# One more GpSimd drain and one TensorE branch hint near the end of a scan-and-experts kernel

## The chip, the cores and the metric

The kernel runs on one core of one Trainium2 chip. Its time is the device time of an execution in microseconds (us). Before the change it is 1088.54 us, the median of three runs. A core has five engines that run their own instruction lists: TensorE (PE in the profile; PEld is its weight load), VectorE (DVE), ScalarE (ACT), GpSimd (POOL) and SyncE (SP). A q behind an engine's name (POOLq, SPq, PEldq) means its sequencer, which reads the list, waits on semaphores, branches and issues transfers. The list itself is fetched from memory by DMA, on the queues that the profile calls "instruction".

## The reference

Two stages. A gated linear recurrence over 4 sequences of 5056 tokens, 256 wide:

```
a_t = exp(8 * sigmoid(r) * log(sigmoid(a_param)))
h   = a_t * h + sqrt(1 - a_t*a_t) * sigmoid(i) * x      (one step per token)
```

Then its output, 20224 rows of 256, goes through a mixture of 8 experts: each token takes the expert with the largest of 8 logits, and its row becomes `gate * (relu(row @ w1[e]) @ w2[e])`, with w1 256 x 1024 and w2 1024 x 256.

## The kernel before

**Front.** The recurrence is done in quads of 512 tokens by ScalarE (gates) and VectorE (scan). Its rows are then sorted by expert: GpSimd writes each row by an indirect DMA (L819, 158 of them) to its expert's part of a buffer in device memory.

**Slots.** The expert stage works in 90 slots of 256 or 128 rows of one expert. Which expert and which rows a slot holds is known at run time alone; SyncE reads it from a table. For a slot, SyncE loads the rows transposed (`xT`), their factors and token numbers (`meta`) and the two weight blocks (`wt`, L969; skipped where the same expert's are there already). TensorE does the first product (`L1`, L1049), ScalarE and VectorE its relu (L1061, L1069), TensorE the second product two slots later (`L2`, L1088 to L1090), ScalarE scales it by the factor `f` that GpSimd has made (L1022, L1096), and GpSimd writes the 128 rows to the output by an indirect DMA (`store`, L1101, 164 of them, one per 128 rows). The weight, `hb`, `ot` and `xT` buffers rotate.

**Order.** A planner of costs and due times (`Plan`) orders these steps; the kernel emits them in its order, and each engine works its list in order.

**The branch.** How many slots of 128 rows the last table fills depends on the data. Sixteen are sure and stand in the plan; code for 19 more stands under `tc.If(used > x["sure"])` (L1219) in `rest()`, which is called ahead of the first product of slot 85 (`late`, with TAIL = 5). Every engine reads `used` (L1218) and takes one of two ways: into the body, or to a short block behind it that raises the semaphores by what the body would have added. In the list of each engine the body lies between the test and that short block; on TensorE it has 2755 instructions. In the executions here the body is not run.

**The end.** Behind the last slot the framework adds a drain on every engine, a barrier, a clearing of semaphores and a second barrier, all put down to L1309. SyncE's part first waits for every transfer.

Of the kernel before, what the change touches and what calls it, by code (L numbers as in the profile page):

```python
# [48 lines left out]
TAIL = 5  # L49
# [483 lines left out]
def lru_moe(ctx, tc, plan, rix, a_in, wg_in, w_in, c_in, id_in, out):  # L533
    nc = tc.nc
    ctx.enter_context(tc.manual_schedule())
    V, A, T, G = nc.vector, nc.scalar, nc.tensor, nc.gpsimd
# [198 lines left out]
    def shape(g):  # L735
        B = sum(plan.quads[z] for z in plan.groups[g])
        return grp[g], B, lambda t: t.unsqueeze(2).to_broadcast([P, B, E])
# [21 lines left out]
    @op  # L759
    def rk(g):  # L760
        o, B, _ = shape(g)
        n = B * E
        pr = o["pr"] = misc[:, 256:256 + 2 * n]
        T.matmul(pr[:, n:2 * n], ones16, flat(o["oh"]), start=True, stop=True)
        T.matmul(pr[:, 0:n], umat, flat(o["oh"]), start=True, stop=True)
# [205 lines left out]
    @op  # L971
    def slot(k):
        o = slots[k]
        ti, j = st["tab", o["z"]]["ti"], o["j"]
        o["r0"] = nc.values_load(ti[:, 1, j:j + 1], engines=[SP], min_val=0, max_val=E * plan.cap,
                                 skip_runtime_bounds_check_because="a row of the buffer")
        o["er"] = nc.values_load(ti[:, 0, j:j + 1], engines=[SP], min_val=0, max_val=E - 1,
                                 skip_runtime_bounds_check_because="an expert")
# [20 lines left out]
    def done_rows(o, i):  # L999
        after(o["c"], i)  # L1000
        if o["e"] is None:
            tc.add_to_no_dep_group("rowload", i.ins)
# [188 lines left out]
    def late_constants():  # L1191

        umat_ = const.tile([P, P], F16, name="umat")
        V.tensor_copy(umat_, cst[:, C_U:C_U + P])
        V.tensor_copy(wg32[:, :, 0:E], wg)

        val_ = const.tile([P, E], F32, name="val")
        V.tensor_copy(val_, cst[:, C_ECAP:C_ECAP + E])
        val9_ = const.tile([1, E + 1], F32, name="val9")
        V.tensor_copy(val9_, cst[0:1, C_ECAP:C_ECAP + E + 1])  # L1200
        for z in range(2):
            nc.sync.dma_start(buf[E * plan.cap + 256 * z:E * plan.cap + 256 * z + 256, :].rearrange("(p j) c -> p j c", j=2), pad)
        return umat_, val_, val9_
# [9 lines left out]
    def rest():  # L1213

        x = plan.orders[-1]
        if x["n"] == x["sure"]:
            return
        used = nc.values_load(st["used"], min_val=0, max_val=x["n"], skip_runtime_bounds_check_because="a count of slots")  # L1218
        with tc.If(used > x["sure"]):  # L1219
            for j in range(x["sure"], x["n"]):  # L1220
                k = len(slots)
                o = dict(k=k, e=None, U=P, J=1, c=x["c"], z=len(plan.orders) - 1, j=j)
                slots.append(o)
                slot(k)
                rw = bass.ds(o["r0"], P)
                meta = small.tile([P, 2], F32, name="last_meta")
                done_rows(o, nc.sync.dma_start(meta, buf[rw, D:D + 2]))
                z = work.tile([P, 2, W], F32, name="in_i", bufs=BUFS["i"]).rearrange("p h w -> p (h w)")
                xT = z[:, 0:D].bitcast(F16).rearrange("p (c u) -> p c u", c=4)
                done_rows(o, nc.sync.dma_start_transpose(xT, buf.bitcast(F16)[rw, 0:2 * D]))  # L1230
                ws, f2 = [], small.tile([P, 1], F32, name="last_f")
                for i in range(2):
                    src = wscr[bass.ds(o["er"], 1), i].rearrange("a p c -> p (a c)")
                    sc = small.tile([P, 1], F32, name=f"last_s{i}")
                    nc.sync.dma_start(sc.bitcast(F16), src[:, 4 * F:4 * F + 2])
                    G.tensor_tensor(f2, f2 if i else meta[:, 0:1], sc, ALU.mult)
                    for y in range(2):
                        t = work.tile([P, 2, W], F32, name="in_x", bufs=BUFS["x"])
                        ws.append(t.rearrange("p h w -> p (h w)").bitcast(F16))
                        nc.sync.dma_start(ws[-1], src[:, 2 * F * y:2 * F * (y + 1)])  # L1240
                h = work.tile([P, 2, W], F32, name="in_r", bufs=BUFS["r"]).rearrange("p h w -> p (h w)").bitcast(F16)
                h = h.rearrange("p (l f u) -> p l f u", l=2, f=NF)
                for g in range(2):
                    p1 = ps_y.tile([P, 2, D], F32, name="yt").rearrange("p a (b u) -> p (a b) u", u=P)
                    gs = slice(4 * g, 4 * g + 4)
                    for i in range(4):
                        fs = slice((4 * g + i) * P, (4 * g + i + 1) * P)
                        for y, (wl, kk, xl) in enumerate(TERMS):
                            T.matmul(p1[:, i], ws[wl].rearrange("p (k f) -> p k f", k=2)[:, kk, fs], xT[:, 2 * xl + kk], start=(y == 0), stop=(y == 5))
                    A.activation(h[:, 0, gs], p1, AF.Relu)  # L1250
                    V.scalar_tensor_tensor(h[:, 1, gs], p1, 0.0, h[:, 0, gs], ALU.max, ALU.subtract)
                for f in range(NF):
                    for y, (l, wl) in enumerate(((0, 0), (0, 1), (1, 0))):
                        T.matmul(misc[:, 0:D], h[:, l, f], ws[2 + wl].rearrange("p (c d) -> p c d", c=NF)[:, f, :],
                                 start=(f == 0 and y == 0), stop=(f == NF - 1 and y == 2))
                A.activation(z[:, D:2 * D], misc[:, 0:D], AF.Copy, scale=f2)
                i = G.indirect_dma_start(
                    out=out[:, :], out_offset=bass.IndirectOffsetOnAxis(ap=meta.bitcast(I32)[:, 1:2], axis=0),
                    in_=z[:, D:2 * D], in_offset=None, bounds_check=plan.tok - 1, oob_is_err=False)
                tc.declare_no_dep(i.ins, group="out", reason="every token has a row of its own")  # L1260
                tc.add_to_no_dep_group("out", i.ins)

    umat = val = val9 = None

    late = next(t for t in plan.ops if t.name == "L1" and t.args == (len(plan.slots) - TAIL, 0))
    for t in plan.ops:
        if t in first:
            continue
        if umat is None and t.eng == "DVE":
            umat, val, val9 = late_constants()  # L1270
        if t is late:
            rest()
        emit[t.name](*t.args)
# [39 lines left out]
```

## Time and profile before

| what | value |
|---|---|
| runs | 1085.17, 1088.54, 1093.79 us |
| profiled execution | 1085.49 us, of which 1083.4 us are the span from first to last instruction |
| mean granted TensorE clock | 0.966 |
| TensorE busy | 981.6 us, 91% of the span |
| GpSimd busy | 428.6 us, 40% |

A busy figure counts matmuls whose ends are modelled, so a TensorE that is 91% busy is not at its peak. Branches, drains and semaphore waits are not counted as busy anywhere; they are found in the answers on one source line, where each has its duration and the start of its first and last.

### The profile page before, as it was taken

Reading aid. Unit: us, or ns where it says so; the run is one execution under the profiler, and the core shown is the slowest. Engines: PE = TensorE matmul, PEld = TensorE weight load, DVE = VectorE, ACT = ScalarE, POOL = GpSimd, SP = SyncE. Lnnn points to the kernel's source line nnn. Section 1 sums busy time; section 2 is a strip of 40 time slices with the busy share of each in tenths; the row PEclk is TensorE's granted clock in tenths of the full one; section 3 lists DMA queues with packets and bytes.
Section 4 is the critical chain, followed back from the end, with each engine's and each line's share of the span. In section 5 each row is a group of like instructions: output and inputs, shape, how many; then the busy total and the mean of one; then the engine's idle time right before and its main releaser. Section 6 shows DMA issues by size and latency. Waiting matters only on the chain. (4 is left out here: it accounts for less than half of the span.)

```text
span 1083.4 us, 23684 instructions
## 1 busy us (share of the span) xinstructions
PE 981.6 (91%) x8790; PEld 863.3 (80%) x8790; DVE 689.4 (64%) x1400; ACT 602.9 (56%) x797; POOL 428.6 (40%) x496
## 2 busy tenths in 40 slices
PE   1328998987999999999999999999999999999985
PEld 1216886866888888888888888888888888889984
DVE  5899897776846576675857768577685663422210
ACT  8766755747455756657476574765746553322221
POOL 0364452251652435345354353544435434122221
PEclk9957998988999999999999999999999999999998
DMA  9968989889899999989999998998999996699951
GB/s 339 403 219 192 313 284 322 245 276 319 282 340 345 343 303 251 357 266 365 328 317 361 269 345 282 299 347 266 335 314 305 361 284 204 193 355 310 248 146 61
DMA packets 170578, 316.67 MB, mean 292 GB/s; under 512 B 119892, under 2 KB 120153, under 8 KB 147930
## 3 DMA queue, kind: packets, MB, share of 16 engines
q1 hardware_dynamic: 155002, 273.50, 81.0%
q0 software_dynamic: 15456, 41.60, 12.4%
q8 instruction: 71, 1.16, 0.5%
q14 instruction: 49, 0.40, 0.1%
HBM read 251.41 MB, written 63.91 MB: 291 GB/s over the span
## 5 line engine op out<-in xcount | busy, mean ns | idle before, releaser
L1049 PE MATMUL p<-xT,wt 128*128 128x256 f16 (+1 forms) x3936 | 417.6, 264 | 3.0 <-SPq L1219 3.0
L1049 PEld LDWEIGHTS <-wt 128*128 128x128 f16 x3936 | 357.4, 99 | 41.9 <-SPq L1219 3.3
L1088 PE MATMUL po<-wt,hb 128*128 128x256 f16 x1184 | 322.8, 273 | 3.3 <-ACT ot L1096 2.7
L1090 PE MATMUL po<-wt,hb 128*128 128x256 f16 x1184 | 322.7, 273 | 0.0
L1089 PE MATMUL po<-wt,hb 128*128 128x256 f16 x1184 | 322.7, 273 | 0.0
L1101 POOL DMA_INDIRECT out<-ot,meta x164 | 186.2, 1135 | 304.6 <-ACT ot L1096 268.7
L1069 DVE SCALAR_TENSOR_TENSOR hb<-p,hb 128x1024 f16<-128x1024 f32 x148 | 180.6, 1221 | 197.7 <-ACT hb L1061 193.5
L1061 ACT ACTIVATE hb<-p 128x1024 f16<-128x1024 f32 (+1 forms) x164 | 167.1, 1019 | 202.6 <-PE p L1049 199.0
L819 POOL DMA_INDIRECT buf<-rows,pi x158 | 172.4, 1091 | 60.3 <-issue 36.8
L1096 ACT ACTIVATE ot<-po,f 128x256 f32<-128x256 f32 x148 | 70.0, 473 | 163.2 <-PE po L1090 150.6
L1088 PEld LDWEIGHTS <-hb 128*128 128x128 f16 x1184 | 115.8, 98 | 17.2 <-issue 4.5
L1089 PEld LDWEIGHTS <-hb 128*128 128x128 f16 x1184 | 115.9, 98 | 17.1 <-issue 4.2
L1090 PEld LDWEIGHTS <-hb 128*128 128x128 f16 x1184 | 115.8, 98 | 13.4
L1022 POOL TENSOR_SCALAR f<-meta,wt,wt 128x2 f32<-128x2 f32 (+1 forms) x82 | 38.3, 467 | 186.1 <-DMA wt<-wscr 139.7
L646 DVE TENSOR_TENSOR_SCAN in_x<-in_r,in_x 128x512 f32<-128x512 f32 (+7 forms) x82 | 96.2, 1181 | 1.4
L627 DVE SCALAR_TENSOR_TENSOR in_x<-in_i,in_x 128x1024 f32<-128x1024 f32 (+1 forms) x38 | 45.8, 1204 | 46.8 <-ACT in_i L622 46.8
L611 DVE SCALAR_TENSOR_TENSOR in_x<-in_i,in_x 128x1024 f32<-128x1024 f32 (+1 forms) x38 | 47.8, 1258 | 39.2 <-ACT in_i L605 20.2
L731 DVE SCALAR_TENSOR_TENSOR rows<-yt,sc,rows 128x256 f16<-128x256 f32 x158 | 66.3, 477 | 6.5 <-ACT rows L724 4.9
L697 PE MATMUL yt<-cst,in_x 128*128 128x128 f32 x316 | 48.7, 299 | 23.3 <-DVE rows L731 8.2
L724 ACT ACTIVATE rows<-yt,sc 128x256 f16<-128x256 f32 x158 | 63.7, 476 | 8.3 <-DVE sc L716 5.3
L1049 PE MATMUL p<-x,wt 128*128 128x256 f32 x256 | 60.9, 394 | 3.1 <-POOL x L1010 3.1
L1086 PE MATMUL po<-wt,hb 128*128 128x256 f32 x256 | 62.5, 397 | 0.5 <-ACT ot L1096 0.4
(110 smaller groups left out, 869.0 us busy)
## 6 DMA issues: line engine op xcount, KB each, us to landing
wt<-wscr SPq DMA_DIRECT2D x164, 1024.5 KB
in_x<-in_rix SPq DMA_DIRECT2D x39, 512.0 KB
in_r<-in_rix SPq DMA_DIRECT2D x37, 512.0 KB
in_i<-in_rix SPq DMA_DIRECT2D x37, 512.0 KB
wscr<-hl SPq DMA_DIRECT2D x16, 1024.5 KB
wt<-in_w SPq DMA_DIRECT2D x16, 1024.0 KB
out<-ot,meta POOLq DMA_INDIRECT x164, 7.0
buf<-pad SPq DMA_DIRECT2D x10, 258.0 KB
```

What stands on the lines that cost most here:

```text
L646: V.tensor_tensor_scan(y[:, lo:hi], av[:, lo:hi], y[:, lo:hi], init, ALU.mult, ALU.add)
L724: A.activation(o["rows"].bitcast(F16)[:, 2 * p + j, 0:D], o["yt", p][:, j], AF.Copy, scale=o["sc"][:, 2 * p + j:2 * p + j + 1])
L731: V.scalar_tensor_tensor(r[:, 2 * p + j, D:2 * D], o["yt", p][:, j], o["sc"][:, 2 * p + j:2 * p + j + 1], r[:, 2 * p + j, 0:D], ALU.mult, ...
L819: i = G.indirect_dma_start(out=buf[:, :], out_offset=bass.IndirectOffsetOnAxis(ap=g["pi"][:, b0 + j:b0 + j + 1], axis=0), in_=rows[q]["row ...
L1049: T.matmul(pv[:, i], wv[:, wl, kk, fs], o["xT"][:, 2 * xl + kk, 0:U], start=(z == 0), stop=(z == len(seq) - 1))
L1061: A.activation(o["h"][:, gs, 0:U] if o["raw"] else o["h"][:, 0, gs, 0:U], o["p1", g], AF.Relu)
L1069: V.scalar_tensor_tensor(o["h"][:, 1, gs, 0:U], o["p1", g], 0.0, o["h"][:, 0, gs, 0:U], ALU.max, ALU.subtract)
L1088: T.matmul(dst, h[:, 0, f, ts], wv[:, 0, f, :], start=(f == 0), stop=False)
L1089: T.matmul(dst, h[:, 0, f, ts], wv[:, 1, f, :], start=False, stop=False)
L1090: T.matmul(dst, h[:, 1, f, ts], wv[:, 0, f, :], start=False, stop=(f == NF - 1))
L1096: A.activation(o["ot", j], o["po", j], AF.Copy, scale=o["f2"][:, j:j + 1])
L1101: i = G.indirect_dma_start(out=out[:, :], out_offset=bass.IndirectOffsetOnAxis(ap=o["id"][j], axis=0), in_=o["ot", j], in_offset=None, bou ...
```

## The change

Three lines have an effect. The test gets the name "few"; a hint for that branch is asked for on TensorE at the step `L2` of slot 83; and GpSimd gets a drain ahead of `store` of slot 85. The assertion (n is 64 at most) adds no instruction.

```
-        with tc.If(used > x["sure"]):
+        with tc.If(used > x["sure"], label="few"):
...
+    full = next(t for t in plan.ops if t.name == "store" and t.args == (len(plan.slots) - TAIL, 0))
+    soon = next(t for t in plan.ops if t.name == "L2" and t.args == (len(plan.slots) - TAIL - 2, 0, 0))
     for t in plan.ops:
...
+        if t is soon:
+            tc.mark_branch_hint_location("few", engines=[mybir.EngineType.PE])
+        if t is full:
+            G.drain()
```

The first rows of TensorE's list, at the start of the program (misc, yt and ls are tiles of the front), before:

```order
L1309 UNCONDITIONAL_BRANCH
L665 MATMUL misc<-in_x,wg_120 32x128 x8
L697 MATMUL yt<-cst,in_x 128x128 x8
L680 MATMUL misc<-cst,ls 128x128
L665 MATMUL misc<-in_x,wg_120 32x128 x8
L680 MATMUL misc<-cst,ls 128x128
```

and with the change:

```order
L1317 UNCONDITIONAL_BRANCH
L1317 BRANCH_PREFETCH_HINT
L665 MATMUL misc<-in_x,wg_120 32x128 x8
L697 MATMUL yt<-cst,in_x 128x128 x8
L680 MATMUL misc<-cst,ls 128x128
L665 MATMUL misc<-in_x,wg_120 32x128 x8
```

The hint does not stand where it was asked for: it is the first instruction of TensorE's list, some 15,200 instructions ahead of the branch, which it names, marked as likely taken. (The step it was asked at comes behind the branch in the plan.) In the built list the taken side of TensorE's test is the short block behind the body. Nothing else in TensorE's list changes but the line numbers.

GpSimd's list between the branch and the end, with the change (a drain is not shown in such a listing):

```order
L1102 DMA out<-ot,meta 20224x256
L1023 TENSOR_SCALAR f_15898<-meta,wt_131,wt_134 128x1
L1102 DMA out<-ot,meta 20224x256
L1023 TENSOR_SCALAR f_15978<-meta,wt_132,wt_135 128x1
L1102 DMA out<-ot,meta 20224x256
L1023 TENSOR_SCALAR f_16069<-meta,wt_2563,wt_2564 128x1
L1102 DMA out<-ot,meta 20224x256
L1023 TENSOR_SCALAR f_16218<-meta,wt_130,wt_133 128x1
L1102 DMA out<-ot,meta 20224x256
L1023 TENSOR_SCALAR f_16237<-meta,wt_131,wt_134 128x1
L1102 DMA out<-ot,meta 20224x256 x3
L1317 UNCONDITIONAL_BRANCH
```

The rows are the stores of slots 82 to 89 and the factors of slots 85 to 89. They stand as before; the new drain is between the factor of slot 87 (f_16069) and the store of slot 85 behind it, so five stores and two factors follow it. It waits for no semaphore and raises none.

## Rows read from the trace of the kernel before

**Rows 1.** Page, busy time by engine.

```profile
PE 981.6 (91%) x8790; PEld 863.3 (80%) x8790; DVE 689.4 (64%) x1400; ACT 602.9 (56%) x797; POOL 428.6 (40%) x496
```

**Rows 2.** Span and clock of the core.

```profile
core 0: 1083.4 us, clock 0.966
```

**Rows 3.** Waits of PE, 1030 to 1084 us: total us, times, longest.

```profile
PE p L1049 <- SPq L1219: 3.0, 1, 3.0
PE po L1088 <- ACT ot L1096: 1.2, 2, 0.6
```

**Rows 4.** Line L1219 (the test): ns min/median/max, first and last start us.

```profile
L1219 SPq EVENT_SEMAPHORE  x9: 17/17/17, 1035.6 to 1036.2; - x9
...
L1219 ACTq COMPARE_BRANCH  x1: 50/50/50, 1031.8 to 1031.8; - x1
...
L1219 PEldq COMPARE_BRANCH  x1: 4217/4217/4217, 1032.3 to 1032.3; - x1
...
L1219 PEldq EVENT_SEMAPHORE  x1: 51/51/51, 1036.6 to 1036.6; - x1
```

**Rows 5.** Timeline around the branch: start us, us, engine, work, [idle before].

```profile
1033.58 0.27 PE L1090 MATMUL po<-wt,hb 128*128 128x256 f16 x1
...
1036.87 4.24 PE L1049 MATMUL p<-xT,wt 128*128 128x128 f16 x48 [3.02 <-SPq L1219]
...
1041.14 1.28 SPq L995 DMA_TRANSPOSE xT<-buf  x1
...
1043.57 2.84 PE L1049 MATMUL p<-xT,wt 128*128 128x128 f16 x48
```

**Rows 6.** Stretches around the branch: busy us of each engine, granted clock, DMA, GB/s.

```profile
1033.85:1036.87 3.02, 0.01 (x1) 0.03 (x1) 0.00 (x0) 0.47 (x1) 1.07 (x2) 0.93 0.01 3
1036.87:1041.11 4.24, 4.24 (x50) 4.23 (x51) 0.00 (x0) 0.00 (x0) 0.28 (x1) 0.65 0.13 35
1041.11:1046.41 5.30, 5.30 (x74) 5.03 (x73) 1.23 (x1) 1.50 (x2) 1.35 (x2) 1.00 0.31 63
```

**Rows 7.** Page, DMA queues: packets, MB, share of 16 engines.

```profile
q8 instruction: 71, 1.16, 0.5%
```

**Rows 8.** DMA queues from 1033.5 to 1035.5 us.

```profile
q8 instruction: 1, 0.02, 4.6%
```

**Rows 9.** Line L1309 (the end), columns as in Rows 4.

```profile
L1309 POOLq EVENT_SEMAPHORE  x4: 17/17/17, 1082.6 to 1083.3; - x4
L1309 POOLq DRAIN  x3: 40/113/10271, 1072.3 to 1083.2; - x3
L1309 SPq DRAIN  x3: 7/7/13, 1075.5 to 1082.8; - x3
```

**Rows 10.** Line L1305 (the start), columns as in Rows 4.

```profile
L1305 POOLq DRAIN  x1: 188/188/188, 0.3 to 0.3; - x1
```

**Rows 11.** Timeline of POOL, 1049 to 1074 us.

```profile
1049.87 1.02 POOL L1101 DMA_INDIRECT out<-ot,meta  x1 [3.89 <-ACT ot L1096]
1050.95 0.33 POOL L1022 TENSOR_SCALAR f<-meta,wt,wt 128x1 f32<-128x1 f32 x1
1055.17 1.02 POOL L1101 DMA_INDIRECT out<-ot,meta  x1 [3.89 <-ACT ot L1096]
1057.74 0.33 POOL L1022 TENSOR_SCALAR f<-meta,wt,wt 128x1 f32<-128x1 f32 x1 [1.56 <-DMA wt<-wscr]
...
1072.55 0.97 POOL L1101 DMA_INDIRECT out<-ot,meta  x1 [2.42 <-ACT ot L1096]
```

**Rows 12.** Timeline of ACT near the end.

```profile
1068.41 0.47 ACT L1096 ACTIVATE ot<-po,f 128x256 f32<-128x256 f32 x1 [2.92 <-PE po L1090]
```

**Rows 13.** Lines L1101 and L819, the indirect DMAs, columns as in Rows 4.

```profile
L1101 POOL DMA_INDIRECT out<-ot,meta x164: 966/982/3172, 107.4 to 1072.5; - x164
...
DMA to landing us min/median/max: 2.5/7.0/9.0
...
L819 POOL DMA_INDIRECT buf<-rows,pi x158: 967/980/2796, 43.4 to 912.9; - x158
```

More of the change, by code (lines that the diff above doesn't have):

```diff
@@ L762, in rk @@
         n = B * E
+        assert n <= 96
         pr = o["pr"] = misc[:, 256:256 + 2 * n]
```

## The prediction, made before the changed kernel was run

> **What bounds the kernel now.** I read the page first. TensorE is busy 91% of the span and no other engine comes near it [rows 1], so the middle of the kernel is paced by matmuls, and two instructions near the end cannot change that part. What they can change are stretches in which TensorE stands still. Therefore I next asked for TensorE's waits from 1030 us on. There are only two kinds: one of 3.0 us, put down to the test for empty slots, and two short ones of 1.2 us together [rows 3]. The answers on the test's own line and on the framework's end then show two instructions that the page does not count as busy.
>
> The first is TensorE's branch. It took 4217 ns from 1032.34 (1032.3 in the row), where ScalarE's took 50 ns [rows 4]. TensorE's last matmul before it ended at 1033.85, the next began at 1036.87 [rows 5]. In that gap DMA was nearly idle (0.01, [rows 6]), and one of the 71 packets of TensorE's instruction queue moved between 1033.5 and 1035.5 [rows 7, 8]. I read this as the fetch of the code behind the branch. The wait is put down to SyncE, since SyncE's nine semaphore steps at L1219 happen to end at 1036.2. I don't believe that: TensorE's own next step, its semaphore instruction, came at 1036.6, right behind the end of its own branch (1032.34 + 4.22 = 1036.56).
>
> The second is GpSimd's drain at the end. It starts at 1072.3 and takes 10271 ns, to 1082.6. SyncE was through all its waits for transfers at 1075.5, when its own drain began, and then stood at the barrier; GpSimd's next step came at 1082.6, and the span ended at 1083.4 [rows 2, 9]. GpSimd's last work, the last store, ended at 1072.55 + 0.97 = 1073.52 [rows 11]. So from 1075.6 to 1082.6 the whole core waits for this drain alone.
>
> **The hint, part by part.** It adds one instruction at the head of TensorE's list, where TensorE has nothing to do yet; itself it costs nothing that can be seen (a semaphore instruction of TensorE takes 51 ns, [rows 4]). If the code behind the branch is in place when the branch is reached, the branch should cost about what ScalarE's did, 50 ns, and it is reached 1033.85 - 1032.34 = 1.5 us before the queued matmuls run out. What is left is from TensorE's semaphore instruction to the first matmul, 1036.87 - 1036.6 = 0.27 us, say 0.3. The gap shrinks by 3.02 - 0.3 = **2.7 us**.
>
> There is a second term, in the clock. In the gap and the matmuls after it the granted clock went 0.93 and 0.65 of full speed (2.4 GHz), so part of that stretch ran at the lower of the two levels; the next stretch is at 1.00 again [rows 6]. The first product behind the gap took 4.24 us, the next one, with the same 48 matmuls, 2.84 [rows 5]. TensorE's short idle pieces later, 0.6 us each, left no such mark. Without the long gap **1.4 us** come back. Together 4.1 us. The bounds are 0 (no hint effect) and 3.02 + 1.4 = 4.4 us. I take 4.1, since 0.27 us is in the same rows.
>
> What is late next is SyncE, which has no hint: its transfers behind the branch still start after 1036.2 [rows 4]. The only one that waited for TensorE there is the `xT` load at 1041.14, for slot 88 [rows 5]. It would be released 4 us earlier, and slot 88's first product is three slots behind slot 85's, about 16 us at 5.3 us a slot [rows 6]. The weight transfers follow TensorE's progress and shift with it. I cost this at nothing.
>
> **The drain, part by part.** Its price is nowhere shown at its place, so I bound it by the four drains of GpSimd that are. The one at the start, ahead of any indirect DMA, took 188 ns [rows 10]; the one at the end, behind 164 + 158 = 322 of them [rows 13], took 10271 ns; the two right behind that took 113 and 40 ns [rows 9]. So the drain is not dear in itself. Either it works off something that the indirect DMAs leave behind and that grows with them, (10271 - 188) / 322 = 31 ns for each, or it pays about 10 us once after any indirect DMA. I take the first, since nothing else in these rows differs by a factor of 50, with the second as a rival.
>
> The new drain has 317 indirect DMAs behind it, 188 + 317 x 31 = 10.0 us. It starts when the factor of slot 87 is done, 1050.95 + 0.33 = 1051.3 [rows 11], and ends at about 1061.3. Queued behind it on GpSimd are the store of slot 85 (1055.17) and the factor of slot 88 (1057.74, [rows 11]). Both come late, the factor by 5 us. Nobody waits for a store but the end and the rotation of `ot` (11 buffers, five stores to come). The factor of slot 88 is read by ScalarE first at 1068.41 [rows 12]: 1068.41 less 1.02 for the store and 0.33 for the factor leaves until 1067.1, so the drain may last 15.8 us before anyone is held up. Its cost on the path is 0; at the upper bound (10.3 us) it is still 0.
>
> The last drain then has five stores behind it: 188 + 5 x 31 = 0.3 us, done at about 1074, before SyncE has seen the last store land. The barrier closes when SyncE arrives, at 1075.6 instead of 1082.6: **7.0 us** less. The bounds are 0 and 7.0; more is not there, because SyncE's waits end no earlier.
>
> "PSUM — Partial Sum Buffer", section "Engine vs sequencer instructions", of the Trainium skill says that a drain waits until its engine is wholly idle. By that rule alone the last drain would have ended with the last store at 1073.5 and an earlier one would gain nothing; the trace has it 9.1 us longer, so the measurement decides.
>
> **Sum.** Against the profiled execution, 1085.49 us: 1085.49 - 4.1 - 7.0 = 1074.4. The median of the runs shown is 3 us above that execution, which gives 1077.4. I put the forecast between them, at 1075.5.
>
> **The rivals.**
>
> *The hint is spent before it is needed.* It stands some 15,200 instructions ahead of its branch. If it only sets off one fetch at the start, those instructions push the fetched code out, and the branch pays its 4.2 us again. For it: 71 packets in 1083 us mean that code is always replaced [rows 7]. Against it: a hint that names a branch can be kept until the branch comes. The time is 1085.49 - 7.0 = 1078.5. This is also the case in which the change does not do what it says, and it has a chance of 0.26.
> The Trainium skill's "Runtime: NRT & Kernel Launch", section "Instruction fetch mechanics", speaks for it: there prefetch is sequential alone, and a taken branch out of the pages at hand waits for a fetch. The packet inside the gap [rows 8] agrees with the second half; of the first half no run shows anything yet.
>
> *The drain has a fixed price.* Then the last one takes its 10 us again, the new one is hidden, and the hint alone counts: 1085.49 - 4.1 = 1081.4. For it: only one drain behind indirect DMAs is on record. Against: 113 and 40 ns right after it. Chance 0.10.
>
> *Neither works*: 1085.5, chance 0.06.
>
> *Slower: the hint keeps a place for the whole run.* If the code it names is held in TensorE's instruction memory from the start, each later piece may be fetched too late, as at the branch. It decides from the point at which a fetch takes longer than the 1.5 us of queued matmuls; then each of at most 71 fetches [rows 7] shows 4.2 - 1.5 = 2.7 us, together 190 us: about 1275 us. Against it: the whole program is laid out so that it is fetched in order, and nothing shows a shortage. Chance 0.03.
>
> **How the numbers follow.** Both parts work: 0.55, 1074.4 to 1077.4, and the forecast is this case's. The runs before lie up to 8 us apart, so about 1% is the least that a measurement here can tell from no change; 1% under the median is 1077.7, right at the edge of this case. I give it 0.62 of being faster by over 1%, the hint's rival 0.1, the others none: 0.34 + 0.03 = 0.37. Slower by over 1% is the last rival and a chance disturbance, 0.04. The rest, 0.59, is within 1%. The range reaches from 1071.5 (this case with its 4.4 us and runs a little under the profiled one) to 1083 (the hint's rival against the slower median, and the drain's rival near 1081.4); the case without any gain and the slow one stay outside.
>
> **What would show it.** Hint: TensorE's branch under 0.3 us, and the gap before the first product of slot 85 at 0.3 us, with that product near 2.8 us and the clock at 1.00. Drain: the long drain moves, a drain of GpSimd of about 10 us between 1047 and 1062 and one under 3 us at the end, with SyncE and GpSimd at the barrier within 1 us of each other. ScalarE must not wait for a factor at slots 88 and 89. I am wrong on the hint if the branch still takes about 4.2 us, on the drain if the last one still takes about 10 us or the new one holds ScalarE.

## The result, and the profile after

| kernel | median | runs | from / to |
|---|---|---|---|
| before | 1091.12 us | 14 | 1085.17 / 1098.83 |
| with the change | 1082.14 us | 14 | 1076.27 / 1087.45 |

The ratio of the two is 0.9911, 95% interval [0.9883, 0.9938]. The change makes the kernel 0.89% faster: 9.7 us of 1091, between 6.8 and 12.8. The sum of the prediction, 1085.5 to 1074.4, was 11.1 us or 1.02%, inside this interval; its forecast of 1075.5 is 13.0 us under the median known then, a little more than the interval allows. Both parts do what was expected of them. The profiled execution took 1076.27 us. An execution over 1.5% above the fastest of its kernel is left out of the ratios; there is one, of the drain alone (1089.61 us). In the changed kernel the lines from 763 on are one higher up to the change, the end is L1317 (L1309 before), and the new drain is L1278.

The page answers to [rows 1] and [rows 7], and the view of the core to [rows 2]:

```profile
PE 978.4 (91%) x8790; PEld 857.9 (80%) x8790; DVE 687.6 (64%) x1400; ACT 600.8 (56%) x797; POOL 426.6 (40%) x496
...
q8 instruction: 70, 1.15, 0.4%
```

```profile
core 0: 1074.2 us, clock 0.965
```

The instruction queue moved one packet less, 70 for 71. The mean clock is the same as before, so the gain is not a change of clock over the whole run.

**The hint.** The waits of TensorE from 1025 us to the end. The 3.0 us of [rows 3] are gone; a wait of 0.3 us, put down to the rows of slot 85, is what is left:

```profile
PE po L1089 <- ACT ot L1097: 1.2, 2, 0.6
PE p L1050 <- DMA xT<-buf: 0.3, 1, 0.3
```

The line of the test answers to [rows 4] (shortest/median/longest in ns, first and last start in us):

```profile
L1220 SPq EVENT_SEMAPHORE  x9: 3/17/487, 1037.6 to 1038.6; - x9
...
L1220 ACTq COMPARE_BRANCH  x1: 50/50/50, 1033.7 to 1033.7; - x1
...
L1220 PEldq COMPARE_BRANCH  x1: 413/413/413, 1034.4 to 1034.4; - x1
...
L1220 PEldq EVENT_SEMAPHORE  x1: 51/51/51, 1035.8 to 1035.8; - x1
```

TensorE's branch takes 413 ns instead of 4217. Its semaphore step at 1035.8 is now ahead of SyncE's nine steps (1037.6 to 1038.6). So TensorE does not wait for those steps, although the list of waits had named SyncE before [rows 3].

The first product of slot 85, in the timeline of TensorE [rows 5], and the stretches around the branch (busy us of PE, PEld, DVE, ACT, POOL, then granted clock, DMA share, GB/s) [rows 6]:

```profile
1036.06 2.84 PE L1050 MATMUL p<-xT,wt 128*128 128x128 f16 x48 [0.30 <-DMA xT<-buf]
```

```profile
1034.36:1035.76 1.40, 1.40 (x13) 1.01 (x11) 1.10 (x1) 0.00 (x0) 0.00 (x0) 1.00 0.54 117
1035.76:1036.06 0.30, 0.01 (x1) 0.03 (x1) 0.00 (x0) 0.21 (x1) 0.00 (x0) 1.00 0.00 0
1036.06:1038.90 2.84, 2.84 (x50) 2.83 (x51) 0.00 (x0) 0.27 (x1) 1.35 (x2) 1.00 0.01 3
```

The gap is 0.30 us instead of 3.02, the product 2.84 instead of 4.24, and the granted clock stays at 1.00 throughout: 2.7 + 1.4 = 4.1 us.

When the code is fetched, the packets of TensorE's instruction queue tell. The hint itself runs at 0.8 us:

```profile
L1317 PEldq BRANCH_PREFETCH_HINT  x1: 50/50/50, 0.8 to 0.8; - x1
```

No packet of that queue moves in the first 50 us of either kernel. Around the branch, from 5 us ahead of its start to 15 us behind it, the packets start at these times:

| kernel | us from the start of TensorE's branch |
|---|---|
| before | -2.5, 1.4, 5.0 |
| with the change | -2.6, 1.2, 9.0 |

So the hint adds no early fetch. One packet about 2.5 us ahead of the branch and one soon behind it stand in both kernels, and the one at 5.0 us is gone. The other 11 kernels with the hint below show the same (-2.4 to -2.7, 1.2 to 1.7, 9.1 to 11.4), the one without it -2.5, 1.4 and 4.7. It would fit this if the hint turned the fetch ahead of the branch to the way that is taken; what a packet holds no trace shows.

**The drain.** The drains of GpSimd, first the new one, then those of the end [rows 9]:

```profile
L1278 POOLq DRAIN  x1: 11871/11871/11871, 1047.5 to 1047.5; - x1
```

```profile
L1317 POOLq EVENT_SEMAPHORE  x4: 17/17/17, 1073.4 to 1074.1; - x4
L1317 POOLq DRAIN  x3: 46/113/2762, 1070.1 to 1073.9; - x3
L1317 SPq DRAIN  x3: 7/7/13, 1073.3 to 1073.6; - x3
```

The long drain has moved. The one at the end now takes 2762 ns, from 1070.1 to 1072.9, and SyncE, with its first drain at 1073.3, is the last at the barrier; GpSimd's step follows at 1073.4. GpSimd around the new drain [rows 11], and ScalarE behind it [rows 12]:

```profile
1048.74 0.33 POOL L1023 TENSOR_SCALAR f<-meta,wt,wt 128x1 f32<-128x1 f32 x1
1060.27 1.02 POOL L1102 DMA_INDIRECT out<-ot,meta  x1 [11.20 <-DMA wt<-wscr]
1061.35 0.33 POOL L1023 TENSOR_SCALAR f<-meta,wt,wt 128x1 f32<-128x1 f32 x1
1061.84 1.02 POOL L1102 DMA_INDIRECT out<-ot,meta  x1 [0.16 <-issue]
...
1070.34 0.98 POOL L1102 DMA_INDIRECT out<-ot,meta  x1 [2.42 <-ACT ot L1097]
```

```profile
1062.81 0.47 ACT L1097 ACTIVATE ot<-po,f 128x256 f32<-128x256 f32 x1 [1.65 <-PE po L1091]
1066.20 0.47 ACT L1097 ACTIVATE ot<-po,f 128x256 f32<-128x256 f32 x1 [2.92 <-PE po L1091]
```

The drain starts at 1047.5 while GpSimd still has a store and a factor to finish, the factor at 1049.07; the drain ends at 1047.5 + 11.9 = 1059.4, so 10.3 us go to the drain alone. (The timeline puts the idle time down to a weight transfer, since drains are not counted as busy.) Beside it TensorE lost nothing, being busy for 10.33 of these 10.33 us:

```profile
1049.08:1059.41 10.33, 10.33 (x143) 9.78 (x141) 2.45 (x2) 3.00 (x4) 0.00 (x0) 1.00 0.79 314
```

The factor of slot 88 comes at 1061.35, and ScalarE uses it at 1066.20, where it waited for TensorE. The last store ends at 1071.32, the span at 1074.2: 2.9 us, where it was 1083.4 - 1073.52 = 9.9. That is the 7.0 us. In this execution the branch was reached 2.0 us later than in that before (1034.4 for 1032.34), from the part of the kernel that neither has changed: 1083.4 - 4.1 - 7.0 + 2.0 = 1074.3, and the span is 1074.2.

### The profile page after: what moved, and what is told of

Its sections match the earlier page's. It is cut to its first block, busy times and chain, and to the rows that moved or that the text cites. A ratio compares the mean times of both kernels' runs of the same rounds, so it can differ in the third digit from the quotient of the medians.

```text
span 1074.2 us, 23686 instructions
## 1 busy us (share of the span) xinstructions
PE 978.4 (91%) x8790; PEld 857.9 (80%) x8790; DVE 687.6 (64%) x1400; ACT 600.8 (56%) x797; POOL 426.6 (40%) x496
## 5 line engine op out<-in xcount | busy, mean ns | idle before, releaser
L1102 POOL DMA_INDIRECT out<-ot,meta x164 | 181.4, 1106 | 317.9 <-ACT ot L1097 260.2
L1023 POOL TENSOR_SCALAR f<-meta,wt,wt 128x2 f32<-128x2 f32 (+1 forms) x82 | 43.1, 526 | 177.6 <-DMA wt<-wscr 127.3
L627 DVE SCALAR_TENSOR_TENSOR in_x<-in_i,in_x 128x1024 f32<-128x1024 f32 (+1 forms) x38 | 45.5, 1198 | 45.2 <-ACT in_i L622 38.2
L611 DVE SCALAR_TENSOR_TENSOR in_x<-in_i,in_x 128x1024 f32<-128x1024 f32 (+1 forms) x38 | 45.8, 1206 | 38.0 <-ACT in_i L605 26.1
```

The costliest lines, as they stand in the source:

```text
L1102: i = G.indirect_dma_start(out=out[:, :], out_offset=bass.IndirectOffsetOnAxis(ap=o["id"][j], axis=0), in_=o["ot", j], in_offset=None, bou ...
```

## The experiments

Runs of one kernel lie up to 14 us apart, more than the effects. Much of that comes ahead of the branch, in the part that no version changes: in the profiled executions here TensorE's branch starts anywhere from 1026.2 to 1034.4 us (the last four runs, on another chip, aside), while from there on the change, the three drains and the hints on all engines, which should end alike, take 39.8 to 39.9 us. So beside each time I read **branch to end**: from the start of TensorE's branch to the end of the span of the profiled execution. It is 1083.4 - 1032.3 = 51.1 us before and 1074.2 - 1034.4 = 39.8 with the change, 11.3 less. Each is read from one execution. All kernels are edits of the changed one, except where the edit says otherwise.

**The hint alone.**

```
-        if t is full:
-            G.drain()
```

> The drain is left out, the hint stays. Theory (two independent gains): TensorE's branch under 0.5 us, gap before slot 85's first product 0.3 us, that product 2.84 us; the last drain of GpSimd again 10 to 12 us; time 4.1 us under the kernel before, about 0.38%. Rival (the hint does nothing and all of the gain is the drain's, or the better gap was chance): branch 4.2 us, gap 3 us, time as before.

Measured: ratio to before 0.9978, interval [0.9962, 0.9994] (12 runs), 2.4 us faster (0.65 to 4.1). The line of the test, and that of the end (L1314 here):

```profile
L1220 PEldq COMPARE_BRANCH  x1: 497/497/497, 1026.2 to 1026.2; - x1
```

```profile
L1314 POOLq DRAIN  x3: 40/113/10272, 1062.1 to 1073.0; - x3
L1314 SPq DRAIN  x3: 7/7/13, 1065.3 to 1072.6; - x3
```

The branch is short again, the gap 0.30 us, the product 2.84 us; the last drain has its 10272 ns back, and the core waits for it as before. Branch to end is 1073.2 - 1026.2 = 47.0 us, 4.1 less than before. So the trace has the 4.1 us in full and nothing given back later; the timed 2.4 us has them at the upper edge of its interval.

**The drain alone.**

```
-        if t is soon:
-            tc.mark_branch_hint_location("few", engines=[mybir.EngineType.PE])
```

> The hint is left out, the drain stays. Theory: TensorE's branch 4.2 us and a gap of 3 us with a first product of 4.2 us behind it; new drain 10 to 12 us, last drain under 3 us; time 7.0 us under the kernel before, about 0.64%. Rival (the gains depend on each other, the drain hides behind a gap): less than 5 us or more than 9 us.

Measured: 0.9939 [0.9919, 0.9959] (11 of 12 runs), 6.6 us faster (4.4 to 8.8). The line of the test, the product behind it, and three stretches from the start of the gap on:

```profile
L1220 PEldq COMPARE_BRANCH  x1: 3917/3917/3917, 1031.6 to 1031.6; - x1
```

```profile
1035.87 4.12 PE L1050 MATMUL p<-xT,wt 128*128 128x128 f16 x48 [2.72 <-PEq L1220]
```

```profile
1033.10:1035.85 2.75, 0.06 (x1) 0.01 (x1) 0.00 (x0) 0.47 (x1) 0.71 (x1) 0.88 0.03 6
1035.85:1038.60 2.75, 2.73 (x26) 2.75 (x27) 0.00 (x0) 0.00 (x0) 0.65 (x2) 0.50 0.16 54
1038.60:1040.10 1.50, 1.50 (x27) 1.48 (x26) 0.00 (x0) 0.06 (x1) 0.00 (x0) 1.00 0.05 1
```

Without the hint the long branch is back, and this time the wait is put down to TensorE's own sequencer (PEq L1220), not to SyncE. The clock term stands apart here: after the gap of 2.72 us, 26 of the 48 matmuls ran at a granted 0.50, the lower level of 1.2 GHz, and the rest at 1.00. Branch to end is 43.7 us, 7.4 less than before; of this the gap (2.72 for 3.02 us) and the product (4.12 for 4.24) were 0.4 shorter by themselves. The two parts alone sum to 4.1 + 7.4 = 11.5 us, beside 11.3 for the change: in the traces they add up, as independent gains do. The timed gains, 0.22% + 0.61% = 0.83% beside 0.89%, agree, but their intervals are too wide to show it.

**The drain without its cover**, ahead of the very last store instead:

```
-    full = next(t for t in plan.ops if t.name == "store" and t.args == (len(plan.slots) - TAIL, 0))
+    full = next(t for t in plan.ops if t.name == "store" and t.args == (len(plan.slots) - 1, 0))
```

> The drain stands one store from the end (ahead of the store of slot 89) instead of five slots. Theory: it starts when the store of slot 88 is done, lasts about 10.3 us, and the last store waits for it: 8 to 9 us slower than the change, about 1083 us of span where the changed kernel's first stretch is as in its profile, so about 2.5 us faster than the kernel before. Rival (the drain runs beside later stores): as the change.

Measured: 0.9983 [0.9963, 1.0002] (12 runs), 1.8 us faster than before, with no change at all inside the interval. The new drain, GpSimd's last two stores, and the end:

```profile
L1278 POOLq DRAIN  x1: 10192/10192/10192, 1064.6 to 1064.6; - x1
```

```profile
1064.79 0.97 POOL L1102 DMA_INDIRECT out<-ot,meta  x1 [2.37 <-ACT ot L1097]
1075.61 0.97 POOL L1102 DMA_INDIRECT out<-ot,meta  x1 [9.85 <-issue]
```

```profile
L1317 POOLq DRAIN  x3: 46/113/2572, 1075.4 to 1079.2; - x3
```

The last drain is short here too, but the long one holds the last store, whose row lies finished, for 9.85 us. Branch to end is 47.4 us, 7.6 more than the change (8 to 9 were expected): of the drain's 7.0 us nothing is left, and 3.7 us of the hint's gain remain. The gain is therefore the place of the drain and the work beside it, not fewer or cheaper drains.

**Three drains**, further ones ahead of the stores of slots 10 and 33. This asks whether the price of a drain goes by the indirect DMAs since the last one:

```
-        if t is full:
+        if t is full or t.name == "store" and t.args in ((10, 0), (33, 0)):
```

> Two more drains of GpSimd, ahead of the stores of slots 10 and 33, behind 65 and 154 indirect DMAs; the third is the change's, behind 317. Theory (31 ns for each indirect DMA since the last drain, or the landing of the last DMA, up to 9 us, where that is later): from the end of GpSimd's work ahead of it the first takes 2 to 9 us, the second 3 to 9 us, the third 163 x 31 ns = 5.2 us where nothing lands late, about half of the 10.3 us that it took alone. Rival 1 (paid once in a program): the first takes 10 us, the third under 1 us or a landing. Rival 2 (a full price each time): the third takes 10.3 us again. The time may rise by some us, since the first two stand in the busy part.

Measured, one run: 1070.71 us, branch to end 39.9. The drains lasted, from the end of GpSimd's work ahead of them, 8.4 us behind 65 indirect DMAs, 8.7 behind 89 and 8.2 behind 163:

```profile
L1278 POOLq DRAIN  x3: 9731/10192/11641, 271.5 to 1042.1; - x3
```

The 163 cost less than the 89, which does not look like 31 ns each. But these drains stand where transfers are in flight, and an indirect DMA can take up to 9.0 us to land ([rows 13]), so this run alone decides neither that nor whether a price is paid once in a program. The next runs do, at the end, where little else is in flight (a DMA share of 0.09 from 1067 to 1071 in the change).

**Drains further ahead of the end**, to read the last drain behind more indirect DMAs (24, 72 and 168). The edit is the slot in `full` alone: 70, 57 and 33.

> The added drain stands ahead of the store of slot 70 instead of 85, so the last drain has 24 indirect DMAs behind it instead of 5; the hint stays. Measured: from the end of the last store's work on GpSimd to the end of the last drain (9.07 us with 322, 1.55 with 5, of which 1.3 to 1.4 is the landing). Theory 31 ns each from the start of the waiting: 24 x 31 = 0.7 us, hidden by the landing, 1.6 us. Second theory, after the run with three drains (a floor of about 6 us once there is more than a handful, and 14 ns each): 6.4 us. Third (full price for more than a handful): 9 us.

> The same ahead of the store of slot 57: 72 indirect DMAs behind the last drain. From the end of the last store's work to the end of the last drain: 31 ns each 2.4 us; floor and 14 ns each 7.1 us; full price 9 us.

> The same ahead of the store of slot 33: 168 indirect DMAs behind the last drain. From the end of the last store's work to the end of the last drain: 31 ns each 5.4 us; floor and 14 ns each 8.4 us; full price 9 us.

Measured, one run each: 1071.3, 1077.99 and 1077.19 us; branch to end 40.2, 43.9 and 43.0 us. The last drain (the longest of three) of each:

```profile
L1317 POOLq DRAIN  x3: 46/113/3540, 1064.9 to 1069.0; - x3
```

```profile
L1317 POOLq DRAIN  x3: 46/113/7164, 1068.0 to 1075.7; - x3
```

```profile
L1317 POOLq DRAIN  x3: 46/113/6342, 1067.9 to 1074.8; - x3
```

Beyond the last store these are 2.3, 6.0 and 5.1 us, which none of the three theories on record gives for all three. A price paid once in a program is out, since 7164 and 6342 ns come behind an earlier drain; 31 ns each are out, since it is dearer behind 72 than behind 168. This is not scatter: behind 5 it took 2762, 2751, 2758 and 2752 ns in four kernels, behind 322 it took 10271 and 10272 in two. A second instruction follows the same order: at the branch GpSimd raises a semaphore of its DMA queue (INC_SWDGE_SEM), in 499, 1466 and 1259 ns in these three kernels, and in 2226 where no drain comes before the branch. From the first two, behind 19 and 67 indirect DMAs, it costs 117 ns and 20 ns for each. Then 163 count as 57 and the 317 as 105, that is 106 and 2 x 106 less. So the backlog seems to fall by 106 now and then.

**Does the backlog fall by 106?** The drain again at other slots (50, 45, 22 and 17), on another chip, where the kernel before took 1108.44 us.

> The drain stands before the store of slot 50, so 96 indirect DMAs lie between it and the last drain, 91 between it and the branch. Theory 'starts over': the backlog that a drain works off grows by about 0.08 us for each indirect DMA and falls to nothing each time about 106 have been issued since the last drain. That figure comes from GpSimd's INC_SWDGE_SEM at the branch, 499 ns behind 19, 1466 behind 67, 1259 behind 163, 2226 behind 317: by the first two, 20 ns each on top of 117 ns, so that 163 count as 57 (106 less) and 317 as 105 (2 x 106 less). 96 are under 106: the last drain ends about 7.9 us after the last store (5.96 at 72, plus 24 x 0.08), and INC_SWDGE_SEM takes about 1.95 us. Rival 'saturates': the backlog grows up to some 70 and then hardly changes until far more: 5.1 to 6.0 us, INC 1.26 to 1.47 us. Time: the change's plus 6 us by the first, plus 3 to 4 by the second; one run can't tell these apart, the drain can.

> The drain stands before the store of slot 45: 120 indirect DMAs to the last drain, 115 to the branch. Theory 'starts over' at about 106: 120 count as 14, 115 as 9, so the last drain ends about 1.9 us after the last store (1.55 at 5, 2.34 at 24) and INC_SWDGE_SEM takes about 0.3 us, although more has been issued than with 96. Rival 'saturates': between the values of 72 and 168, so 5.1 to 6.0 us and 1.26 to 1.47 us. By 31 ns each, the price that the prediction took, 188 + 120 x 31 = 3.9 us of drain.

> The drain stands before the store of slot 22: 208 indirect DMAs to the last drain, 203 to the branch. Theory 'starts over' at about 106: they count as 102 and 97, just under the second start, so the last drain ends about 8.4 us after the last store and INC_SWDGE_SEM takes about 2.07 us. Rival 'saturates': between the values of 168 and 322, about 6 us and 1.5 us. By 31 ns each 188 + 208 x 31 = 6.6 us of drain.

> The drain stands before the store of slot 17: 232 indirect DMAs to the last drain, 227 to the branch. Theory 'starts over' at about 106, so a second time at about 212: they count as 20 and 15, the last drain ends about 2.1 us after the last store, and INC_SWDGE_SEM takes about 0.42 us; the time is then the change's. Rival 'saturates': about 6.7 us and 1.6 us, the time 5 us above the change's. By 31 ns each 188 + 232 x 31 = 7.4 us of drain.

Measured, one run each: 1095.47, 1087.29, 1096.67 and 1103.74 us. Branch to end: 45.8, 39.9, 46.3 and 40.1 us. The last drain and the semaphore of each, in this order:

```profile
L1317 POOLq DRAIN  x3: 46/113/9119, 1083.5 to 1093.2; - x3
...
L1220 POOLq INC_SWDGE_SEM  x1: 1946/1946/1946, 1047.8 to 1047.8; - x1
```

```profile
L1317 POOLq DRAIN  x3: 46/112/3170, 1081.2 to 1085.0; - x3
...
L1220 POOLq INC_SWDGE_SEM  x1: 2426/2426/2426, 1045.8 to 1045.8; - x1
```

```profile
L1317 POOLq DRAIN  x3: 46/113/9604, 1084.2 to 1094.4; - x3
...
L1220 POOLq INC_SWDGE_SEM  x1: 2066/2066/2066, 1048.4 to 1048.4; - x1
```

```profile
L1317 POOLq DRAIN  x3: 46/113/3383, 1097.5 to 1101.5; - x3
...
L1220 POOLq INC_SWDGE_SEM  x1: 419/419/419, 1061.9 to 1061.9; - x1
```

All last drains, sorted by the indirect DMAs since the drain before. "Left" takes off 106 for each fall (one from 120 on, two from 232 on). The last drain starts 1.2 us before GpSimd's last store instruction ends in all of these, so the duration less 1.2 us is how long it lasts beyond that store:

| since the last drain | left | last drain, ns | beyond the last store, us | branch to end, us |
|---|---|---|---|---|
| 1 (ahead of the last store) | 1 | 2572 | 1.4 | 47.4 |
| 5 (the change) | 5 | 2762 | 1.55 | 39.8 |
| 24 | 24 | 3540 | 2.3 | 40.2 |
| 72 | 72 | 7164 | 6.0 | 43.9 |
| 96 | 96 | 9119 | 7.9 | 45.8 |
| 120 | 14 | 3170 | 2.0 | 39.9 |
| 168 | 62 | 6342 | 5.1 | 43.0 |
| 208 | 102 | 9604 | 8.4 | 46.3 |
| 232 | 20 | 3383 | 2.2 | 40.1 |
| 322 (hint alone) | 110 | 10272 | 9.1 | 47.0 |

Sorted by "left", the durations rise without exception, from 2572 to 10272 ns; by the first column they do not. All four last drains came out as "starts over" had them (7.9, 1.9, 8.4 and 2.1 us expected), against 5 to 7 us by the rival. One step of that theory failed: the semaphore behind 115 took 2426 ns instead of 0.3 us, which is 117 + 115 x 20.1. So in that run the fall comes between 115 and 120 indirect DMAs after the added drain, not at 106, and takes off 106 then. What sets either number no run shows.

The added drains themselves, in the middle of the kernel, fit less well. They count from the program's start, and beyond GpSimd's last work ahead of them they took 8.6 us behind 90, 5.9 behind 114, 4.6 behind 154, 10.1 behind 202, 7.8 behind 226, 7.4 behind 250, 9.2 behind 298 and 10.3 behind 317. Most are dearer than the same number left is at the end; how much of that is transfers in flight no run separates. One is cheaper:

```profile
L1278 POOLq DRAIN  x1: 7087/7087/7087, 414.3 to 414.3; - x1
```

With all 114 left it would cost over 9 us, so counted from the program's start a fall seems to come earlier than behind an added drain. The table is therefore a rule for the last drain alone.

The last column is the bill. Up to 2.0 us beyond the last store the drain is hidden, since SyncE's own first drain comes 1.98 us behind that store in the change (1073.3 - 1071.32). Every us beyond goes to the end: 6.0 - 2.0 = 4.0 behind 72, and 43.9 - 39.8 = 4.1 was measured.

**Hints on all five engines**, to see whether SyncE, which I had costed at nothing, comes next:

```
-            tc.mark_branch_hint_location("few", engines=[mybir.EngineType.PE])
+            tc.mark_branch_hint_location("few", engines=[mybir.EngineType.PE, mybir.EngineType.SP, mybir.EngineType.Activation, mybir.EngineType.DVE, mybir.EngineType.Pool])
```

> The hint is asked for on all five engines; the drain stays. Theory (TensorE's fetch was the only one on the path): SyncE's nine semaphore steps follow its branch by under 1 us instead of 2.8, TensorE's gap stays at 0.3 us, time as the change, within 0.3 us of what the same run would have without it. Rival (SyncE's late loads cost something later): 1 to 3 us faster than the change.

Measured: 0.9904 [0.9873, 0.9935] (6 runs); branch to end 1067.8 - 1027.9 = 39.9 us.

```profile
L1220 SPq EVENT_SEMAPHORE  x9: 17/17/17, 1028.9 to 1030.7; - x9
...
L1220 SPq COMPARE_BRANCH  x1: 73/73/73, 1028.4 to 1028.4; - x1
```

SyncE takes its first step 0.5 us after its branch, where it was 1037.6 - 1034.8 = 2.8 us with the change. Nothing follows from it: branch to end is the change's. SyncE's fetch is off the path. No version here is faster than the change by more than these comparisons can tell.

## Why the prediction was right, step by step

- **The branch costs a fetch, and the hint takes it away.** Right. Every kernel with the hint shows 413 to 503 ns, the two without it 4217 and 3917. The term "about 50 ns" was too low by a factor of 8 to 10; it cost nothing, because the queued matmuls cover 1.4 us in the changed kernel. The prediction read the packet inside the gap [rows 8] as the fetch; that row alone did not show it, since with the hint a packet moves at the same place.
- **SyncE is not what TensorE waits for** [rows 3]. Right: with the change SyncE's steps come after TensorE's.
- **2.7 us of gap and 1.4 us of clock.** Both right in the traces (0.30 and 2.84 us in the changed kernel, 47.0 for 51.1 us from branch to end with the hint alone). By time the hint alone was 2.4 us, with 4.1 at the edge of the interval.
- **The hint is spent before it is needed** (0.26). Refuted. It runs at 0.8 us, at the head of the list, and the branch is still short 1.03 ms later; nor does it set off a fetch when it runs, since no packet moves in the first 50 us. The rule of the Trainium skill that spoke for this rival ("Runtime: NRT & Kernel Launch", section "Instruction fetch mechanics": prefetch is sequential alone) does not hold for a hinted branch here, which took 413 ns; what it says of an unhinted one, a wait for a fetch, agrees with the 4217 ns and with one packet more (71 for 70, in both kernels without the hint against all 12 with it).
- **31 ns for each indirect DMA.** This step was wrong, and harmless. It gave 10.0 us for the new drain, which took 10.3. That was luck twice over: 322 and 317 happen to leave 110 and 105, both near the most that was seen left (115), and at the end 102 to 110 left cost 8.4 to 9.1 us, so part of the 10.3 is something else, which no run separates. In the last drain what is left costs about 0.08 us each from 24 on ((10.27 - 3.54) / (110 - 24)), about half of that below, and 106 of them fall away without a drain. For the last drain the step gave 0.3 us; it took 1.55 beyond the last store. SyncE's 1.98 us hid that.
- **The new drain is covered.** Right: it ended at 1059.4, the factor of slot 88 was there at 1061.35 + 0.33 = 1061.7, and ScalarE used it at 1066.20 without a wait for it. What it costs without cover, the drain ahead of the last store shows.
- **The barrier closes when SyncE arrives, 7.0 us earlier.** Right to a tenth.
- **A fixed price** (0.10) and **a place kept for the whole run** (slower, 0.03). Both refuted, the first by the 2762 ns, the second by a time that fell and by 70 packets where there were 71.
- **The absolute time** was low: 1075.5 for a median of 1082.14, which lies 0.9 us under the upper end of the range, where the prediction had put its rivals. The time alone could not have told the cases apart; the traces do. The profiled execution (1076.27) is the fastest of its 14, and the kernel before had a median of 1091.12 in the same comparison, 2.6 us above the runs first shown. I placed the forecast between profiled run and median; the median alone would have been nearer.

## What to carry to other kernels

Look for instructions that the busy figures leave out, branches and drains, and read where the span ends from the last two engines at the barrier. Work that the end would do alone may be done ahead, where its engine has slack and nobody reads what is queued behind it; five slots from the end it was free, one slot from the end it cost all it had saved. Where the runs scatter by more than the effect, compare executions from a common mark close to the change (here the branch), not from their start.

## What I had not expected of the hardware

- The price of GpSimd's last drain is a sawtooth in the indirect DMAs since the drain before it: 9119 ns behind 96, 3170 behind 120, 9604 behind 208, 3383 behind 232. By it, a kernel whose end happens to lie just behind such a fall would need no further drain; that was not tried.
- INC_SWDGE_SEM reads the same backlog at 117 + 20.1 ns for each left: 499, 1466, 1946, 2426 ns behind 19, 67, 91 and 115, and 419, 1259, 2066 and 2226 behind 227, 163, 203 and 317.
- After a gap of 2.7 us TensorE ran 26 matmuls at a granted 0.50. The idle pieces of 0.3 and 0.6 us in the changed kernel left no such mark: the granted clock is 1.00 from 1060 to 1067.
- A branch hint at the head of TensorE's list made a branch 1.03 ms later short without an early fetch: about 2.5 us ahead of the branch a packet moves with the hint and without it.
